# A bank of PSUM for every result from a list, and a new list of steps: attention and a feed-forward layer on one Trainium2 core

## The chip, the core and the metric

The kernel runs on one core of a Trainium2 chip. Its engines work side by side, each through its own list of instructions in order: TensorE (PE) multiplies matrices and writes only to PSUM, VectorE (DVE) and ScalarE (ACT) read PSUM and SBUF, GpSimd (POOL) works on SBUF, and SyncE (SP) issues nearly all DMAs. PSUM has 128 partitions and eight banks of 512 float32 values per partition; a result of a matmul here takes one bank or part of one. The metric is the device time of one execution in microseconds (us).

## The reference

`q`, `k` and `v` are (4, 8, 768, 64): four batches, eight heads, 768 positions. Attention sees a band of local positions and a few global ones, with a bias that grows with the distance; its output, 768 rows of 512 for each batch, goes through a layer norm and a feed-forward layer with a residual:

```python
scores = scale * np.matmul(q, k.transpose(0, 1, 3, 2))
keep = is_global | is_local                      # rel in [0, n_local) or key < n_global
scores = np.where(keep, scores + bias, -1e9)
a = softmax(scores)
x = (a @ v) as (B, S, H*D)                       # 4 x 768 x 512
xn = (x - mean) / sqrt(var + 1e-6) * g_ln
out = x + np.maximum(xn @ w_ch1, 0.0) @ w_ch2    # 512 -> 2048 -> 512
```

## The kernel before

The 24 tiles of 128 rows (four batches of six) are taken in an order of their own: the first tile of each batch comes first (tiles 0 to 3, float32 matmuls of 64 or 128 rows, function `first`), then the other 20 in pairs (`attention`, float16 parts, high and low). The feed-forward layer needs each weight as two float16 parts. `weight` loads 16 blocks of 1 MB, and each goes through two steps on ACT (L380, L388), two on DVE (L384, L392), a cast, and a subtraction (L403) that gives the low part. A product of high and low parts is three matmuls. Tiles 0 to 3 take their first layer alone in 16 results of 48 matmuls (`ffn1_alone`, L764 to L766); then come pairs with 256 columns (`ffn1`, L792 to L794), and from pair 4 on a scheme with seven products in place of eight (`seven`, L817 to L819, and `both_`, L954 and L973). `ffn2` (L1053) is the second layer of the early tiles.

Every piece of work is entered in a plan as a step on one engine with what it reads and writes. The order of the steps is a list of numbers, `STEPS`, and which engine takes a step that can go to several is a list, `HOMES`; both are written out in the file. The plan turns them into the instruction lists of the engines. Buffers (places in SBUF, banks in PSUM) are rings: the next user of a place waits until all users of the previous one are done.

PSUM's banks before are fixed by the kind of result, in turn: scores take banks 0 and 1 (`SS`), the outputs of attention banks 2 and 3, later 2 alone (`PVS`, `PVS2`), the first layer 4 and 5, later also 3 (`F1S`, `F1S2`), the second layer 6 and 7, and the transposes of the first tiles 6, 7 and 4 (`FLIPS`). The ring goes by the order in which the program enters the results.

At the start, while inputs and weights are on their way, PE gets fillers: matmuls of 252 columns on a constant tile, `still`, into the upper part of bank 3 (`hold`, L1174). Where the plan has PE free for a while and the planned time is under `HOLD`, it puts as many fillers there as fill 0.9 of the gap at 0.108 us each. They compute nothing that is used.

A flag that tells whether all ranges are in bounds is worked out near the end (`checks`, L1132 on PE, L1119 to L1122 on DVE); the steps after it stand in a block of their own, and a slower second kernel behind it (from L1427 on) runs only if the flag is set.

Of the kernel before, what the change touches and what calls it, by code (L numbers as in the profile page):

```python
# [18 lines left out]
ALU = mybir.AluOpType  # L19
# [4 lines left out]
B, H, S, D = 4, 8, 768, 64  # L24
DM, DF = 512, 2048
P = 128
NT = S // P
NK = DM // P
# [58 lines left out]
class Plan:  # L87
# [4 lines left out]
    def __init__(self):  # L92
        self.ops, self.wrote, self.read, self.rings, self.group = [], {}, {}, {}, None
# [55 lines left out]
    def order(self):  # L149
        for bufs, made in self.rings.values():  # L150
            for old, new in zip(made, made[bufs:]):
                for o in new.users:
                    if not any(p in new.users for p in o.before):
                        self.edges(old.users, o)
        assert sorted(STEPS) == list(range(len(self.ops)))
        self.planned = self.times([self.ops[n] for n in STEPS])
# [24 lines left out]
def banded(ctx, tc, q, k, v, n_global, n_local, g_ln, w1, w2, out, flag):  # L181
# [8 lines left out]
    plan = Plan()  # L190
# [56 lines left out]
    def psum(tag, of, shape):  # L247
        n_ = turn(tag, of)
        return plan.at([("ps", n_)], lambda: shaped(banks[n_], shape))
# [354 lines left out]
    def attention(t):  # L604
# [27 lines left out]
        for g_ in range(H // gh):  # L632
# [4 lines left out]
            def score(ps=ps, heads=heads):  # L637
                for u, h in enumerate(heads):
                    for n_ in range(nb):
                        for a in range(2):  # L640
                            pe.matmul(ps()[:, u, n_ * P:(n_ + 1) * P], lhsT=qT()[:, a * H + h, :], rhs=use[n_][0]()[:, h, :], start=(a == 0), stop=(a == 1))  # L641
# [112 lines left out]
    def ffn1_alone(t, j):  # L754
# [4 lines left out]
        def emit():  # L759
            for a in range(4):  # L760
                fs = slice((4 * j + a) % 8 * P, ((4 * j + a) % 8 + 1) * P)
                for kk in range(NK):
                    wh, wl = (block(j // 2, kk // 2)[:, part, kk % 2, fs] for part in range(2))
                    pe.matmul(ps()[:, a], lhsT=wh, rhs=xT()[:, 0, kk, :], start=(kk == 0), stop=False)  # L764
                    pe.matmul(ps()[:, a], lhsT=wh, rhs=xT()[:, 1, kk, :], start=False, stop=False)
                    pe.matmul(ps()[:, a], lhsT=wl, rhs=xT()[:, 0, kk, :], start=False, stop=(kk == NK - 1))  # L766
# [351 lines left out]
    def raised(pf):  # L1118
        vec.tensor_scalar(out=fine[:, 0:1], in0=pf()[:, 0:1], scalar1=float(P), scalar2=None, op0=ALU.is_ge)  # L1119
        vec.tensor_scalar(out=fine[:, 1:3], in0=pf()[:, 1:3], scalar1=1.0, scalar2=None, op0=ALU.is_ge)  # L1120
# [3 lines left out]
    def checks():  # L1124
# [6 lines left out]
        pf = plan.at([("ps", F1S2[0])], lambda: banks[F1S2[0]][0:1, 0:3])  # L1131
        op("PE", 0.1, lambda: pe.matmul(pf(), lhsT=ones, rhs=sums, start=True, stop=True), r=["ones", "sums"], w=[pf])  # L1132
# [83 lines left out]
IDLE, HOLD, FILL = 3, 130.0, 0.9  # L1216
# [15 lines left out]
HOMES = {32: 1, 50: 1, 53: 1, 68: 1, 115: 1, 147: 1, 153: 2, 154: 1, 167: 2, 175: 1, 182: 1, 188: 1, 189: 1, 196: 1, 203: 1, 210: 1, 230: 2, 231: 1,  # L1232
# [304 lines left out]
```

## Time and profile before

| | |
|---|---|
| time, median of 3 runs | 598.55 us (597.78 to 598.64) |
| the profiled execution: time, span | 598.57 us, 596.8 us (1.77 us lie around the span) |
| PE busy | 586.7 us, 98% of the span |
| DVE, ACT, POOL busy | 501.9 (84%), 334.1 (56%), 218.2 us (37%) |
| granted clock of PE, mean | 0.997 |
| fillers (L1174) | 151, the last at 52.9 us |
| all DMA queues | 91.74 MB, mean 154 GB/s |

A row of a matmul gives its start and a modelled end, and the next one starts long before that end: rows of 128 columns are 0.22 us long and start 0.055 us apart. So the busy share of PE hides gaps that are shorter than a row, and what PE really does is read from the starts.

### The profile page before, as it was taken

What the parts mean: (1) busy time and instruction counts of PE and PEld (TensorE: products, weight loads), DVE (VectorE), ACT (ScalarE), POOL (GpSimd) and SP (SyncE); (2) the same over time, 40 slices, a digit from 0 to 9 for tenths busy, and PEclk for the clock granted to TensorE, in tenths of its full rate; (3) what the DMA queues carried; (4) which work ended last, traced back from release to release, by engine and by line L of the source; (5) the groups of instructions that cost most, each with busy time, mean ns of one, the idle gap of its engine ahead of it and who ended that gap; (6) DMA issues with size and microseconds to landing.
All of it is one profiled execution on the core that took longest, in us unless ns stands there. A gap on an engine that the chain in (4) does not pass through costs nothing.

```text
span 596.8 us, 18645 instructions
## 1 busy us (share of the span) xinstructions
PE 586.7 (98%) x7657; PEld 513.6 (86%) x7657; DVE 501.9 (84%) x1147; ACT 334.1 (56%) x819; POOL 218.2 (37%) x228
## 2 busy tenths in 40 slices
PE   9899999999999999999999999999999999999995
PEld 7889988556877856899999999999999999999995
DVE  3999999989979988988987998888887997778661
ACT  4989788865644553753753762753664663551210
POOL 1315443245454253462332541341662441351200
PEclk9999999999999999999999999999999999999998
DMA  8896999996953878887989989978978796642201
GB/s 246 253 311 146 238 248 224 229 177 131 154 107 71 151 131 163 134 173 158 168 169 167 169 154 146 150 142 162 183 135 167 125 177 126 111 79 46 66 2 58
DMA packets 260269, 91.74 MB, mean 154 GB/s; under 512 B 250192, under 2 KB 250448, under 8 KB 260176
## 3 DMA queue, kind: packets, MB, share of 16 engines
q1 hardware_dynamic: 259888, 90.47, 77.0%
q8 instruction: 62, 1.02, 0.7%
q14 instruction: 31, 0.25, 0.2%
q10 hardware_dynamic: 288, 0.00, 0.0%
HBM read 38.01 MB, written 6.29 MB: 74 GB/s over the span
## 4 chain that ended last, share of the span: by engine, by line
PE 92%; DVE 4%; DMA 2%; ACT 1%; issue 0%; SPq 0%; DVEq 0%
PE bank L973 14%; PE bank L1053 14%; PE bank L954 12%; PE bank L817 8%; PE bank L819 8%; PE bank L818 8%; PE bank L641 6%; PE bank L794 2%; PE bank L792 2%; PE bank L793 2%; PE bank L1174 2%; PE bank L468 2%; PE bank L470 2%; PE bank L469 2%; PE bank L766 2%; PE bank L764 2%
## 5 line engine op out<-in xcount | busy, mean ns | idle before, releaser
L203 ACT ACTIVATE arena<-arena 128x512 f16<-128x512 f32 (+3 forms) x115 | 69.3, 619 | 54.3 <-DVE arena L716 13.8
L973 PE MATMUL bank<-w2h,arena 128*128 128x256 f16 x512 | 93.3, 273 | 0.0
L203 ACT ACTIVATE arena<-bank 128x512 f16<-128x512 f32 (+1 forms) x95 | 55.3, 591 | 67.1 <-PE bank L819 39.6
L819 PE MATMUL bank<-arena 128*128 128x128 f16 x512 | 87.9, 219 | 0.0
L818 PE MATMUL bank<-arena 128*128 128x128 f16 x512 | 87.9, 219 | 0.0
L817 PE MATMUL bank<-arena 128*128 128x128 f16 x512 | 87.9, 219 | 0.0
L505 ACT ACTIVATE arena<-arena,mn 128x256 f32<-128x256 f32 x160 | 80.0, 501 | 3.7
L1053 PE MATMUL bank<-w2h,arena 128*128 128x512 f16 x256 | 81.7, 379 | 0.0
L973 PEld LDWEIGHTS <-arena 128*128 128x128 f16 x768 | 73.0, 98 | 7.7
L973 PE MATMUL bank<-w2l,arena 128*128 128x256 f16 x256 | 69.8, 273 | 0.0
L954 PEld LDWEIGHTS <-arena 128*128 128x128 f16 x672 | 63.9, 98 | 6.8
L1053 PEld LDWEIGHTS <-arena 128*128 128x128 f16 x384 | 36.0, 98 | 37.4
L819 PE MATMUL bank<-arena,w 128*128 128x128 f16 x384 | 66.7, 219 | 0.0
L817 PE MATMUL bank<-arena,w 128*128 128x128 f16 x384 | 66.7, 219 | 0.0
L818 PE MATMUL bank<-arena,w 128*128 128x128 f16 x384 | 66.7, 219 | 0.0
L500 DVE CUSTOM_DVE_ANT_0 arena<-bank,mask 128x256 f32<-128x256 f32 x160 | 60.1, 417 | 7.4 <-PE bank L641 3.4
L647 POOL TENSOR_TENSOR arena<-arena 128x512 f16<-128x512 f32 x39 | 45.1, 1160 | 42.9 <-DVE r L476 10.6
L817 PEld LDWEIGHTS <-arena 128*128 128x128 f16 x512 | 50.1, 98 | 0.3
L818 PEld LDWEIGHTS <-arena 128*128 128x128 f16 x512 | 50.1, 98 | 0.3
L819 PEld LDWEIGHTS <-arena 128*128 128x128 f16 x512 | 50.1, 98 | 0.0
L1053 PE MATMUL bank<-w2l,arena 128*128 128x512 f16 x128 | 48.5, 379 | 0.0
L641 PE MATMUL bank<-kT,qT 128*128 128x128 f16 x640 | 47.2, 219 | 0.3 <-DMA qT<-qT 0.3
(215 smaller groups left out, 1773.1 us busy)
## 6 DMA issues: line engine op xcount, KB each, us to landing
arena<-in_moe_w_ch_dram SPq DMA_DIRECT2D x16, 1024.0 KB, 6.9
kf<-in_k_dram SPq DMA_DIRECT2D x28, 256.0 KB, 4.7
vf<-in_v_dram SPq DMA_DIRECT2D x28, 256.0 KB, 4.2
qf<-in_q_dram SPq DMA_DIRECT2D x24, 256.0 KB, 4.5
out_dram<-x SPq DMA_DIRECT2D x23, 256.0 KB, 2.5
qT<-qT SPq DMA_DIRECT2D x40, 128.0 KB, 3.5
pT<-arena SPq DMA_TRANSPOSE x80, 3.4
arena<-arena SPq DMA_TRANSPOSE x36, 3.2
```

Source lines behind the costliest of these rows:

```text
L203: act.activation(out=out(), in_=src(), func=AF.Relu if relu else AF.Copy, scale=by)
L468: pe.matmul(pv[:, h, :], lhsT=ph, rhs=vv[:, h, :D], start=(n_ == 0), stop=False)
L500: vec.tensor_tensor_reduce(out=T()[:, u, :], in0=ps()[:, u], in1=mask(h), scale=1.0 / Z, scalar=3e38, op0=ALU.add, op1=ALU.min, accum_out= ...
L505: act.activation(out=T()[:, u, :], in_=T()[:, u, :], func=AF.Exp, scale=-1.0, bias=mn()[:, h:h + 1], accum_out=sm()[:, h:h + 1])
L641: pe.matmul(ps()[:, u, n_ * P:(n_ + 1) * P], lhsT=qT()[:, a * H + h, :], rhs=use[n_][0]()[:, h, :], start=(a == 0), stop=(a == 1))
L647: pick(pair(lambda eng, pn=pn, T=T: eng.tensor_tensor(out=pn()[:, :, 1, :], in0=T(), in1=pn()[:, :, 0, :], op=ALU.subtract), 512, "PD"), r ...
L817: pe.matmul(ps()[:, i, :], lhsT=wh, rhs=xT()[:, hi + kk, :], start=(first_ and i == 0 and kk == 0), stop=False, skip_group_check=True)
L818: pe.matmul(ps()[:, i, :], lhsT=wh, rhs=xT()[:, lo + kk, :], start=False, stop=False, skip_group_check=True)
L819: pe.matmul(ps()[:, i, :], lhsT=wl, rhs=xT()[:, hi + kk, :], start=False, stop=(i == 3 and kk == 1), skip_group_check=True)
L954: pe.matmul(ps(), lhsT=hh()[:, part, f, :], rhs=rhs, start=first_ and f == 0 and k == 0, stop=(f == 3 and k == 2), skip_group_check=True)
L973: pe.matmul(ps(), lhsT=hh()[:, part, i, :], rhs=w[:, f + i, n * K2:(n + 1) * K2], start=False, stop=(i == 3 and k == 2), skip_group_check= ...
L1053: pe.matmul(ps[t](), lhsT=h[:, part, :], rhs=w[:, f + a, :], start=(f + a == 0 and n_ == 0), stop=(f + a == NF - 1 and n_ == 2))
```

## The change

Each result in PSUM, in the order in which the program enters it, gets its bank from a list `BANKS` of 257 numbers from 0 to 7. The ring of a bank is then ordered by the place of its results in `STEPS`, no longer by the order of entry. `STEPS` and `HOMES` are replaced as a whole. Since results that share a bank are now written from one `start` flag, scores and `ffn1_alone` set it on the first matmul of a bank only, and the check's small product takes the first row of a full buffer. `HOLD` goes from 130 to 75.

```diff
     def order(self):
-        for bufs, made in self.rings.values():
+        rank = {self.ops[n]: m for m, n in enumerate(STEPS)}
+        for key, (bufs, made) in self.rings.items():
+            if key[0] == "ps":
+                made = sorted((b for b in made if b.users), key=lambda b: min(rank[o] for o in b.users))
             for old, new in zip(made, made[bufs:]):
...
     def psum(tag, of, shape):
-        n_ = turn(tag, of)
-        return plan.at([("ps", n_)], lambda: shaped(banks[n_], shape))
+        n_ = BANKS[len(plan.banked)]
+        b = plan.at([("ps", n_)], lambda: shaped(banks[n_], shape))
+        plan.banked.append(b)
+        return b
...
-                            pe.matmul(ps()[:, u, n_ * P:(n_ + 1) * P], lhsT=qT()[:, a * H + h, :], rhs=use[n_][0]()[:, h, :], start=(a == 0), stop=(a == 1))
+                            pe.matmul(ps()[:, u, n_ * P:(n_ + 1) * P], lhsT=qT()[:, a * H + h, :], rhs=use[n_][0]()[:, h, :], start=(u == 0 and n_ == 0 and a == 0), stop=(u == gh - 1 and n_ == nb - 1 and a == 1), skip_group_check=True)
...
-        pf = plan.at([("ps", F1S2[0])], lambda: banks[F1S2[0]][0:1, 0:3])
+        pf = psum("pf", F1S2, [P, 3])
...
-IDLE, HOLD, FILL = 3, 130.0, 0.9
+IDLE, HOLD, FILL = 3, 75.0, 0.9
...
+BANKS = [
+    4, 1, 6, 2, 4, 7, 1, 0, 5, 3, 5, 3, 1, 7, 6, 4, 4, 7, 5, 2, 5, 7, 2, 1, 4, 6, 7, 5, 1, 7, 1, 3, 0, 3, 2, 5, 6, 2, 1, 5, 4, 5, 7, 0, 0, 6, 0, 2, 7, 1,
...
 STEPS = [
-    3, 2, 8, 5, 19, 23, 10, 6, 7, 9, 0, 1, 22, 21, 148, 141, 24, 25, 27, 155, 20, 80, 79, 17, 162, 84, 4, 12, 26, 13, 14, 28, 31, 33, 29, 15, 34, 32,
...
+    9, 7, 23, 81, 19, 5, 6, 8, 3, 2, 1, 0, 21, 22, 79, 80, 141, 27, 25, 4, 28, 12, 26, 29, 41, 13, 31, 33, 30, 14, 15, 16, 32, 42, 34, 87, 45, 89, 46,
```

The lists move instructions on every engine. Below stand three places, first as it was and then as it is. Names carry the bank (`bank6_78` is bank 6) and the tile; the new file's lines are 3 to 5 higher here (L197 is L200, L440 is L445).

PE, the third of the first loads (`q` and `k` of tile 2 are transposed, L440, the scores of tile 0 multiplied, L539, and its mask added, L543), before:

```order
L440 MATMUL bank6_78<-arena_71,qf2_0_128 128x128 x4
L539 MATMUL bank0_72<-k0_0_165,q0_0_187 128x128 x4
L440 MATMUL bank4_76<-arena_71,kf2_0_132 128x128 x4
L543 LDWEIGHTS arena_71
L543 MATMUL bank0_72<-arena_71 128x128
```

And changed:

```order
L445 MATMUL bank6_78<-arena_71,kf2_0_129 128x128 x4
L544 MATMUL bank1_73<-k0_0_189,q0_0_168 128x128 x4
L445 MATMUL bank2_74<-arena_71,qf2_0_133 128x128 x4
L544 MATMUL bank4_76<-k0_0_189,q0_0_168 128x128 x4
L548 LDWEIGHTS arena_71
L548 MATMUL bank1_73<-arena_71 128x128
```

Before, the second half of tile 0's scores (L539) comes after tile 1's and uses bank 0 again; now it follows at once in bank 4. Along the whole list of PE, the fillers fall from 151 to 72; up to the first matmul of `ffn1_alone` there are 148 before and 70 now, and all other matmuls of the main program are the same in number and shape.

DVE, the first reductions of the scores (L549) and what stands between them, before:

```order
L199 TENSOR_SCALAR q0_1_228<-bank6_78 128x512
L549 TENSOR_REDUCE nm0_236<-bank0_72 128x4
L549 TENSOR_REDUCE nm1_262<-bank1_73 128x4
L549 TENSOR_REDUCE nm0_236<-bank0_72 128x4
L197 COPY pT0_0_285<-bank7_79 128x512
L384 TENSOR_SCALAR arena_71<-arena_71 128x1024
```

And changed:

```order
L202 TENSOR_SCALAR q0_1_244<-bank2_74 128x512
L554 TENSOR_REDUCE nm0_260<-bank1_73 128x4
L554 TENSOR_REDUCE nm0_260<-bank4_76 128x4
L554 TENSOR_REDUCE nm1_288<-bank0_72 128x4
L200 COPY k0_2_292<-bank5_77 128x512
L554 TENSOR_REDUCE nm1_288<-bank7_79 128x4
L200 COPY pT0_1_312<-bank1_73 128x512
L389 TENSOR_SCALAR arena_71<-arena_71 128x1024
```

Before, three reductions come out of two banks; now four come out of four. The first step on a weight (L384, now L389) moves from fifth to seventh behind the copy of `q`.

SP, the loads after the first two, before:

```order
L269 DMA qf2_0_128<-in_q_dram 128x8x64
L269 DMA kf2_0_132<-in_k_dram 128x8x64
L372 DMA arena_71<-in_moe_w_ch1_dram 128x2x512 x2
L520 DMA vf1_124<-in_v_dram 128x8x64
L372 DMA arena_71<-in_moe_w_ch1_dram 128x2x512
L520 DMA vf0_122<-in_v_dram 128x8x64
L269 DMA qf1_0_185<-in_q_dram 128x8x64
L269 DMA kf1_0_193<-in_k_dram 128x8x64
```

And changed:

```order
L274 DMA kf2_0_129<-in_k_dram 128x8x64
L274 DMA qf2_0_133<-in_q_dram 128x8x64
L274 DMA kf1_0_135<-in_k_dram 128x8x64
L274 DMA qf1_0_137<-in_q_dram 128x8x64
L377 DMA arena_71<-in_moe_w_ch1_dram 128x2x512 x2
L525 DMA vf0_121<-in_v_dram 128x8x64
L377 DMA arena_71<-in_moe_w_ch1_dram 128x2x512
L525 DMA vf1_116<-in_v_dram 128x8x64
```

`q` and `k` of the third tile (0.25 MB each) move ahead of the first two weights (1 MB each). At the other end of SP's list the last DMA of the main program was half a row block of tile 23 (L991, 128 KB) and is a whole one of tile 22 (L998, 256 KB); PE's last products were tile 23's and are tile 22's.

## Rows read from the trace of the kernel before

**Rows 1.** The page: busy time, share of the span and instructions of each engine.

```profile
PE 586.7 (98%) x7657; PEld 513.6 (86%) x7657; DVE 501.9 (84%) x1147; ACT 334.1 (56%) x819; POOL 218.2 (37%) x228
```

**Rows 2.** Windows, PE alone: stretch, PE busy, granted clock, DMA share, GB/s.

```profile
0.00:25.00 25.00, 22.49 (x173) 1.00 0.89 253
25.00:50.00 25.00, 24.44 (x266) 1.00 0.87 246
50.00:75.00 25.00, 24.29 (x381) 1.00 0.93 219
75.00:150.00 75.00, 75.00 (x840) 1.00 1.00 200
450.00:575.00 125.00, 125.00 (x1850) 1.00 0.55 103
```

**Rows 3.** Waits of PE: line, waited for, us in total, times, longest.

```profile
PE bank L1174 <- DVE x L579: 1.5, 2, 1.0
PE bank L766 <- POOL w L403: 0.4, 1, 0.4
PE bank L641 <- DMA qT<-qT: 0.3, 1, 0.3
```

**Rows 4.** Timeline of PE: start, us, line, count; start, middle and end of the span.

```profile
0.98 3.75 PE L1174 MATMUL bank<-still 128*128 128x252 bf16 x17 [0.98 <-DVE still L1205]
4.68 1.09 PE L440 MATMUL bank<-arena,kf 128*128 128x128 f32 x4
5.56 1.59 PE L1174 MATMUL bank<-still 128*128 128x252 bf16 x9
6.99 0.60 PE L440 MATMUL bank<-arena,qf 128*128 128x128 f32 x4
7.43 1.15 PE L1174 MATMUL bank<-still 128*128 128x252 bf16 x9
...
29.98 2.02 PE L1174 MATMUL bank<-still 128*128 128x252 bf16 x17
31.84 0.63 PE L440 MATMUL bank<-arena,kf 128*128 128x128 f32 x4
...
44.64 0.22 PE L764 MATMUL bank<-arena,w 128*128 128x128 f16 x1
44.69 0.22 PE L765 MATMUL bank<-arena,w 128*128 128x128 f16 x1
44.75 0.22 PE L766 MATMUL bank<-arena,w 128*128 128x128 f16 x1
...
77.06 0.38 PE L1053 MATMUL bank<-w2l,arena 128*128 128x512 f16 x1
77.28 0.59 PE L1053 MATMUL bank<-w2h,arena 128*128 128x512 f16 x2
...
590.24 0.27 PE L973 MATMUL bank<-w2h,arena 128*128 128x256 f16 x1
```

**Rows 5.** The chain that ended last, two of its links: start, us, engine, line, count.

```profile
551.96 2.62 PE bank L954 x24
586.58 3.94 PE bank L973 x36
```

**Rows 6.** Timeline of DVE: waits for PE at the start, six rows in sequence, the last weight.

```profile
10.94 0.69 DVE L549 TENSOR_REDUCE nm<-bank 128x4 f32<-128x512 f32 x1 [0.67 <-PE bank L543]
13.12 0.69 DVE L549 TENSOR_REDUCE nm<-bank 128x4 f32<-128x512 f32 x1 [1.48 <-PE bank L543]
14.75 0.69 DVE L549 TENSOR_REDUCE nm<-bank 128x4 f32<-128x512 f32 x1 [0.94 <-PE bank L543]
...
43.49 1.26 DVE L403 TENSOR_TENSOR w<-arena,w 128x1024 f16<-128x1024 f32 x1
44.66 1.33 DVE L384 TENSOR_SCALAR arena<-arena 128x1024 uint16<-128x1024 uint16 x1
45.78 0.66 DVE L549 TENSOR_REDUCE nm<-bank 128x4 f32<-128x512 f32 x1
46.36 0.67 DVE L197 COPY pT<-bank 128x512 f32<-128x512 f32 x1
...
120.13 1.23 DVE L403 TENSOR_TENSOR w2l<-arena,w2h 128x1024 f16<-128x1024 f32 x1
```

**Rows 7.** The page, DMA issues of the output: count, KB each, median us to landing.

```profile
out_dram<-x SPq DMA_DIRECT2D x23, 256.0 KB, 2.5
out_dram<-x SPq DMA_DIRECT2D x2, 128.0 KB, 1.7
```

More of the change, by code (lines that the diff above doesn't have):

```diff
@@ L92, in __init__ @@
     def __init__(self):
-        self.ops, self.wrote, self.read, self.rings, self.group = [], {}, {}, {}, None
+        self.ops, self.wrote, self.read, self.rings, self.group, self.banked = [], {}, {}, {}, None, []
     def ring(self, name, bufs, make):
@@ L763, in emit @@
                     wh, wl = (block(j // 2, kk // 2)[:, part, kk % 2, fs] for part in range(2))
-                    pe.matmul(ps()[:, a], lhsT=wh, rhs=xT()[:, 0, kk, :], start=(kk == 0), stop=False)
-                    pe.matmul(ps()[:, a], lhsT=wh, rhs=xT()[:, 1, kk, :], start=False, stop=False)
-                    pe.matmul(ps()[:, a], lhsT=wl, rhs=xT()[:, 0, kk, :], start=False, stop=(kk == NK - 1))
+                    pe.matmul(ps()[:, a], lhsT=wh, rhs=xT()[:, 0, kk, :], start=(a == 0 and kk == 0), stop=False, skip_group_check=True)
+                    pe.matmul(ps()[:, a], lhsT=wh, rhs=xT()[:, 1, kk, :], start=False, stop=False, skip_group_check=True)
+                    pe.matmul(ps()[:, a], lhsT=wl, rhs=xT()[:, 0, kk, :], start=False, stop=(a == 3 and kk == NK - 1), skip_group_check=True)
         names = [f"1_{j}_{c_}{e}" for c_ in range(2) for e in "hl"]
@@ L1118, in raised @@
     def raised(pf):
-        vec.tensor_scalar(out=fine[:, 0:1], in0=pf()[:, 0:1], scalar1=float(P), scalar2=None, op0=ALU.is_ge)
-        vec.tensor_scalar(out=fine[:, 1:3], in0=pf()[:, 1:3], scalar1=1.0, scalar2=None, op0=ALU.is_ge)
+        vec.tensor_scalar(out=fine[:, 0:1], in0=pf()[0:1, 0:1], scalar1=float(P), scalar2=None, op0=ALU.is_ge)
+        vec.tensor_scalar(out=fine[:, 1:3], in0=pf()[0:1, 1:3], scalar1=1.0, scalar2=None, op0=ALU.is_ge)
         vec.tensor_reduce(out=every, in_=fine, axis=AX.X, op=ALU.min)
@@ L1130, in checks @@
         op("DVE", 0.5, verdict, r=[("mv", t) for t in range(B * NT)], w=["ok", "sums"])
-        pf = plan.at([("ps", F1S2[0])], lambda: banks[F1S2[0]][0:1, 0:3])
-        op("PE", 0.1, lambda: pe.matmul(pf(), lhsT=ones, rhs=sums, start=True, stop=True), r=["ones", "sums"], w=[pf])
+        pf = psum("pf", F1S2, [P, 3])
+        op("PE", 0.1, lambda: pe.matmul(pf()[0:1, 0:3], lhsT=ones, rhs=sums, start=True, stop=True), r=["ones", "sums"], w=[pf])
         op("DVE", 0.6, lambda: raised(pf), r=[pf], w=["flag"])
@@ L1231 @@
 SUMS = (*G, list(range(20, 24)))
-HOMES = {32: 1, 50: 1, 53: 1, 68: 1, 115: 1, 147: 1, 153: 2, 154: 1, 167: 2, 175: 1, 182: 1, 188: 1, 189: 1, 196: 1, 203: 1, 210: 1, 230: 2, 231: 1,
[19 rows of a table removed]
+HOMES = {26: 1, 28: 1, 32: 1, 56: 1, 75: 1, 88: 1, 147: 1, 153: 2, 154: 1, 160: 2, 161: 1, 175: 1, 189: 1, 203: 1, 217: 1, 231: 1, 263: 1, 272: 1,
[19 rows of a table added]
+BANKS = [
[5 rows of a table added]
+]
 TMPS = [28, 27]
```

218 rows, old and new, of tables (BANKS, HOMES, STEPS) are left out of this document.

## The prediction

> **What bounds the kernel now.** I read the busy times first: PE is busy for 98% of the span, DVE for 84% [rows 1]. [...] Third, the waits of PE: three rows of DVE, POOL and DMA that together are 2.2 us [rows 3], in a span of 597. Fourth, the starts of single matmuls, since the modelled ends cover gaps. A matmul of 128 columns follows the one before by 0.055 to 0.06 us, one of 512 by 0.22 [rows 4], and 24 of 256 take 2.62, or 0.109 each [rows 5]. In the chain the last 36 stand end to end (3.94 us) [rows 5].
>
> With these I add up what PE has to do, the fillers left out: 4096 matmuls of 128 columns by 0.0556, 228 us; 1824 of 256 by 0.109, 199; 384 of 512 by 0.216, 83; 960 of 64 by 0.029, 28; and 27 us for the float32 transposes and products of the first four tiles and their masks. That is 564 us, and the change leaves all of it. PE's last matmul starts at 590.24 [rows 4] and so ends its issue at 590.35. PE therefore lost 26 us: 16.2 to 151 fillers (31.84 less 29.98 for 17 of them is 0.109 with rounding [rows 4]; 0.107 over all), and 10 to standing still. Since the windows have no gap after 75 us, nearly all of the 26 lie before that. This is the whole prize; what happens to banks at 300 us can only cost.
>
> **What lost the 26 us.** At the start there is no work: PE starts at 0.98, waits for the first load until 4.68 with 17 fillers between (1.9 us still), and stands 0.44 and 0.45 us around the next nine fillers [rows 4], in all 3.7 us. Afterwards it waits on results in few banks: scores of four half tiles go through banks 0 and 1, and a filler that writes bank 3 waits for DVE to read an attention result out of the same bank, 1.5 us in two waits [rows 3]. DVE waits for PE in turn, 0.67, 1.48 and 0.94 us in three rows [rows 6].
>
> **The change, part by part.**
>
> Fillers: 151 become 72, that is 79 by 0.107, 8.5 us off PE's list. They are free only if work takes their place or the wait behind them goes; that is the rest of the sum. The lowered `HOLD` takes none away by itself: the last stands far below 75 us in both lists.
>
> Start: the three first blocks of fillers (17, 9 and 9) and the three first loads are as they were in number and size, so the 3.7 us and 3.8 us of fillers stay. Then the changed list puts 24.0 us of real work ahead of the first matmul of `ffn1_alone`, with 70 fillers (7.5 us); before it is 21.2 us of work and 148 fillers (15.9), and the matmul starts at 44.64 [rows 4]. The work moved up is the transposes and scores of tile 2, whose loads go ahead of the weights. SP's list is moved by 0.5 MB, at the 253 GB/s of the first window [rows 2] 2 us for the first two weights. I cost this at nothing, since DVE reaches the first step of the first weight 1.2 us later in its new list anyway (two rows of 0.6); if the cover is gone, it is the 2 us.
>
> The pace of the weights: this is the term I can bound from both sides. DVE has to work through its list in order until the low part of the last of 16 weights is there. I add the list up to that row with the distances of starts: 1.15 for a subtraction or shift of 1024, 1.11 for the first step, 0.6 for an eviction, a reduction or a copy of 512 [rows 6], and so on. Before it comes to 104.6 us, changed to 105.2. Before, the row ends at 121.3 [rows 6], so DVE had not worked for 16.7 us, 5.5 of them before its inputs came. PE first reads this weight after 97.6 us of real work before, 123.6 with the 26 lost: it was ready 2.3 us earlier. In the changed list 105.4 us of real work stand ahead of it. If DVE idles for D, the weight is ready at 105.2 + D, and PE must have lost at least D - 0.2 by then. D as before gives 16.5 us lost. The lower end does not come from DVE: the 7.7 us of the 72 fillers and the 3.7 of the start are 11.4. I take 14, the middle, because the three waits of DVE for PE [rows 6], 3.1 us, are just those that more banks dissolve (16.7 less 3.1 is 13.6), while ACT's part of each weight stays what it was.
>
> The later stretch: PE had no gap there [rows 2], so no bank can give anything; I cost it at nothing. Whether it takes something I counted from the lists: places after the first 100 us where PE writes a bank again with under 1.5 us of its own work since the matmuls that the reader of the bank waited for. There are 52 before and 35 now. Two readers of 512 columns are 0.67 us each [rows 6], so these are the places that could stall; before they did not. If the cover is gone, one costs about 0.5 us. The moves of casts between ACT, DVE and POOL change DVE's total by some rows in 1147; DVE has 16% of the span free [rows 1].
>
> The end: from PE's last matmul to the end of the span are 6.45 us. The last DMA now has 256 KB in place of 128, which land after 2.5 in place of 1.7 us [rows 7]: plus 0.8, bounded by 0 and 0.9.
>
> The sum against the profiled execution (596.8 us of span, 598.57 in all, 0.02 above the median): 564 of work, 14 lost, 6.45 of end, 0.8 more, and 1.77 around the span: **587.0 us**, 11.6 less.
>
> On the clock the rows show 1.00 in the first window too, where PE was busy for 22.49 of 25 us with its fillers [rows 2]. [...]
>
> **The rivals.**
>
> (A) DVE sets the pace as before: the weights are no earlier than their sum allows with the same 16.7 us of idling. For it speaks that DVE's sum is the same to 0.6 us and that it was at work for 90% of that stretch; against it, that part of its idling was for PE. PE loses 16.5: 589.5 us. A variant is that PE stands still for 10 us as before beside the fewer fillers: 17.7 lost, 590.7.
>
> (B) All of the fillers turn into waits, since what they covered is the arrival of loads: the bytes are the same and DMA runs at 89% in the first window [rows 2]. PE loses 26 again and the end is longer: 599.4 us, no change by the bound. Against it: more real work stands ahead of the same loads.
>
> [...]
>
> (D) Slower: short turnarounds stall at last. 35 places by 0.5 us are 17.5 us, 604.5; it decides above 0.33 us per place. Against it are the 52 places of before without a gap.
>
> (E) The lists don't do what they say because a wait is hidden in a ring: the banks' rings now go by the place in `STEPS`, so no result can wait for a later one. I give it no chance of its own.
>
> **How the numbers follow.** Forecast 0.57 (583 to 589.2), A 0.26, B 0.07, C 0.05, D 0.05. The low end is the floor of 11.4 us lost without the longer DMA: 583.6, rounded down by 0.6 for what the sum of 564 may be off. The high end takes in A and its variant and 2 us for the first weights, up to 593.5. Less than 0.2% (1.2 us) can't be told from no change. Faster by more than that are the forecast and A, and a part of B, C and D where the fall is small: 0.86; same: most of B, 0.05; slower: C and D and the rest of B, 0.09.
>
> **What the profile would show.** If right: the first matmul of `ffn1_alone` starts at 35 to 38 us instead of 44.64; the row of the last weight's low part ends at 117 to 120; PE's windows are full from about 75 us; PE's last matmul is at 576 to 580, with a granted clock of 1.00 in the first window. A is right if that DVE row ends at 121 to 122 and PE waits for it. B would show the first `ffn1_alone` at 44 again with waits on DMA or DVE where the fillers were. [...] The forecast is wrong if PE has a gap after 150 us, or if the last matmul comes later than 583.

## The result, and the profile after

The changed kernel takes 589.28 us (median of four: 590.48, 589.69, 588.87, 588.65) against 598.31 beside it, a ratio of 0.9852 with an interval of 0.9833 to 0.9871. Timed again later it took 590.00 (ratio 0.9870, 0.9845 to 0.9895). The forecast was 587.0 with a range of 583.0 to 593.5: direction and range hold, and the median is 2.3 to 3 us later.

The page and PE's windows of the changed kernel, which answer to [rows 1, 2]. The profiled execution is the slowest of the four: 590.48 us, 588.7 of them span.

```profile
PE 578.9 (98%) x7578; PEld 507.2 (86%) x7578; DVE 498.5 (85%) x1149; ACT 333.6 (57%) x818; POOL 222.5 (38%) x227
```

```profile
0.00:25.00 25.00, 23.91 (x189) 1.00 0.92 243
25.00:50.00 25.00, 23.23 (x266) 0.93 0.87 274
50.00:75.00 25.00, 25.00 (x446) 1.00 0.75 202
75.00:150.00 75.00, 75.00 (x762) 1.00 0.98 201
150.00:300.00 150.00, 149.50 (x1816) 1.00 0.85 150
300.00:450.00 150.00, 150.00 (x2237) 1.00 0.91 159
```

PE is full from 50 us on but for half a microsecond near 293, where before it was not until 75. One stretch is new: from 25 to 50 us it is busy for 23.23 us only, and the granted clock is 0.93, where before it was 1.00. PE's own rows show where (columns as in [rows 4]; lines after the new code are 3 to 12 higher than before, so L764 is L769 here):

```profile
36.25 0.22 PE L769 MATMUL bank<-arena,w 128*128 128x128 f16 x1
...
38.93 1.95 PE L572 MATMUL bank<-vf,pT 128*128 128x65 f32 x16
42.33 0.66 PE L445 MATMUL bank<-arena 128*128 128x128 f32 x4 [1.45 <-ACT arena L206]
...
42.99 0.31 PE L771 MATMUL bank<-arena,w 128*128 128x128 f16 x1
43.10 0.31 PE L769 MATMUL bank<-arena,w 128*128 128x128 f16 x1
43.21 0.31 PE L770 MATMUL bank<-arena,w 128*128 128x128 f16 x1
...
581.95 0.27 PE L978 MATMUL bank<-w2h,arena 128*128 128x256 f16 x1
```

The first matmul of `ffn1_alone` comes at 36.25 instead of 44.64. Those 8.4 us are the gain: PE's last matmul is 8.3 us earlier. But some four microseconds after 36.25 PE stands still for 1.45 us for tile 2's normed row, whose transposes are L445, and then its matmuls follow each other by 0.107 us instead of 0.055, while the granted clock is 0.50. The windows bound that stretch:

```profile
40.00:42.00 2.00, 0.88 (x8) 1.00 0.97 358
42.00:44.00 2.00, 1.67 (x16) 0.71 1.04 397
44.00:46.00 2.00, 2.00 (x22) 0.50 0.83 242
46.00:48.00 2.00, 2.00 (x36) 0.93 0.12 32
```

The wait near 293 us is one for a bank that DVE has to read first:

```profile
293.08 0.27 PE L959 MATMUL bank<-w2h,arena 128*128 128x256 f16 x1 [0.50 <-DVE x L485]
```

PE's last matmul starts at 581.95 (590.24 before) and the span ends 6.64 us after its issue. With 564 us of work, PE lost 18.1 us, where it lost 26 before and 14 were forecast.

What PE waits for stands on three engines, in the order of time: DVE's row that takes off the mean and multiplies by the gain (L595), POOL's power (`rs`, 128 elements of one column), ACT's scaling with it. DVE in its turn then waits for ACT's step on the next weight.

```profile
38.15 0.97 DVE L595 SCALAR_TENSOR_TENSOR arena<-x,mv,gb 128x512 f32<-128x512 f32 x1
39.04 2.45 DVE L389 TENSOR_SCALAR arena<-arena 128x1024 uint16<-128x1024 uint16 x2
...
43.43 1.23 DVE L397 SCALAR_TENSOR_TENSOR arena<-arena 128x1024 int32<-128x1024 int32 x1 [1.95 <-ACT arena L393]
```

```profile
34.30 4.27 POOL L408 TENSOR_TENSOR w<-arena,w 128x1024 f16<-128x1024 f32 x2
38.52 3.00 POOL L497 TENSOR_TENSOR rs<-rs,half 128x1 f32<-128x1 f32 x1
```

```profile
41.56 0.72 ACT L206 ACTIVATE arena<-arena,rs 128x512 f32<-128x512 f32 x1 [1.92 <-POOL rs L497]
```

The power takes 3.00 us; the other 23 rows of the same line take 0.55 to 1.10. It ends at 41.52, just after DVE's two 16-bit steps L389 (41.49).

Earlier, DVE still waits for PE to finish scores, three times as before [rows 6]:

```profile
14.43 0.69 DVE L554 TENSOR_REDUCE nm<-bank 128x4 f32<-128x512 f32 x1 [1.27 <-PE bank L548]
...
16.32 0.69 DVE L554 TENSOR_REDUCE nm<-bank 128x4 f32<-128x512 f32 x1 [0.61 <-PE bank L548]
...
19.85 0.69 DVE L554 TENSOR_REDUCE nm<-bank 128x4 f32<-128x512 f32 x1 [0.51 <-PE bank L548]
```

### The profile page after: what moved, and what is told of

The parts are those of the page before. It is cut to its first block, busy times and chain, and to the rows that moved or that the text cites. A ratio compares the mean times of both kernels' runs of the same rounds, so it can differ in the third digit from the quotient of the medians.

```text
span 588.7 us, 18462 instructions
## 1 busy us (share of the span) xinstructions
PE 578.9 (98%) x7578; PEld 507.2 (86%) x7578; DVE 498.5 (85%) x1149; ACT 333.6 (57%) x818; POOL 222.5 (38%) x227
## 4 chain that ended last, share of the span: by engine, by line
PE 90%; DVE 2%; issue 0%; ACT 0%; DVEq 0%
PE bank L1058 14%; PE bank L978 14%; PE bank L959 12%; PE bank L822 8%; PE bank L824 8%; PE bank L823 8%; PE bank L646 6%; PE bank L770 2%; PE bank L798 2%; PE bank L799 2%; PE bank L797 2%; PE bank L771 2%; PE bank L769 2%; PE bank L473 2%; PE bank L475 2%; PE bank L474 1%
## 5 line engine op out<-in xcount | busy, mean ns | idle before, releaser
L206 ACT ACTIVATE arena<-arena 128x512 f16<-128x512 f32 (+3 forms) x120 | 73.4, 624 | 71.6 <-DVE arena L838 16.6
L978 PE MATMUL bank<-w2h,arena 128*128 128x256 f16 x512 | 92.7, 273 | 0.0
L206 ACT ACTIVATE arena<-bank 128x512 f16<-128x512 f32 (+1 forms) x85 | 49.5, 593 | 48.3 <-PE bank L824 26.1
L652 POOL TENSOR_TENSOR arena<-arena 128x512 f16<-128x512 f32 x42 | 48.5, 1159 | 53.7 <-ACT arena L206 15.2
L959 PE MATMUL bank<-w2h,arena 128*128 128x256 f16 x256 | 47.1, 273 | 0.5 <-DVE x L485 0.5
```

Source lines behind the costliest of these rows:

```text
L206: act.activation(out=out(), in_=src(), func=AF.Relu if relu else AF.Copy, scale=by)
L652: pick(pair(lambda eng, pn=pn, T=T: eng.tensor_tensor(out=pn()[:, :, 1, :], in0=T(), in1=pn()[:, :, 0, :], op=ALU.subtract), 512, "PD"), r ...
L959: pe.matmul(ps(), lhsT=hh()[:, part, f, :], rhs=rhs, start=first_ and f == 0 and k == 0, stop=(f == 3 and k == 2), skip_group_check=True)
L978: pe.matmul(ps(), lhsT=hh()[:, part, i, :], rhs=w[:, f + i, n * K2:(n + 1) * K2], start=False, stop=(i == 3 and k == 2), skip_group_check= ...
```

## The experiments

Theory at the start: the gain is the start-up (real work in place of fillers and waits), and the 2 to 3 us over the forecast are this wait and the half clock behind it. Rival: DVE's pace of the weights sets the end (A of the prediction). Medians of the kernel before lie at 598.18 to 598.21 in all of them.

**The power ahead of POOL's subtraction.** `STEPS.remove(161); STEPS.insert(STEPS.index(128) + 1, 161)`, and `HOLD` 40 for 75, which takes away the last two fillers.

> Only one step moves: on POOL the power of tile 2's moments goes ahead of the second of the two 2.1 us subtractions that stood before it (the low part of block w1_1_0), and the two fillers planned at 47 us are gone (70 left). Theory (the lost time is the wait at 40.7 us and the lower clock after it): the power starts when DVE has the moments, at about 37.5, and takes 0.6 to 1.3 us as in its other rows; the transposes of xT2 follow the products of tile 1 or 2 without the 1.6 us of standing still; the granted clock stays at 1.00 from 42 to 47 us (it was 0.50); PE's lost sum falls from 18.1 to about 14.5, the last matmul comes at 578.5, the time is 585.8 +- 0.8. Rival A (DVE's pace of weights sets the end): the gain is no more than the last weight's low part comes earlier (DVE itself waited 1.95 us for ACT at 43.4), so at most 2 us, 587.4 to 589.3, and PE stands still for that weight near 118 to 121 us. A third reading, that the power is slow wherever it stands beside any DVE work: it still takes about 3 us and nothing changes (589.3).

589.71 us, ratio 0.9854 (0.9840 to 0.9867): no gain. The power is short now, but DVE's next row is not (DVE, then POOL):

```profile
38.30 2.70 DVE L595 SCALAR_TENSOR_TENSOR arena<-x,mv,gb 128x512 f32<-128x512 f32 x1
```

```profile
37.78 0.55 POOL L497 TENSOR_TENSOR rs<-rs,half 128x1 f32<-128x1 f32 x1 [1.15 <-ACT arena L206]
38.30 2.15 POOL L408 TENSOR_TENSOR w<-arena,w 128x1024 f16<-128x1024 f32 x1
```

L595 takes 2.70 us instead of 0.97: it starts with the subtraction and ends 0.55 us after it. The wait has changed hands, and PE still stands 0.82 us at the same place. It also met waits for DVE at 45.5 and 48.9 us (0.19 and 0.20 us) that were not there before: it was ahead of two low parts that DVE makes, tile 2's and that of weight w1_1_1.

**DVE's two 16-bit steps later.** Steps 164, 171, 165, 172 and 166 go behind 133 (xT2's low part, that of tile 2's transposed row); `HOLD` 40.

> POOL's list stays; DVE's two first steps (16-bit, 1.2 us each) of weights w1_1_1 and w1_2_0 go behind the low part of xT2 (with them ACT's and DVE's next steps of these two weights), and the two fillers planned at 47 us are gone. Nothing of DVE then stands beside POOL's power at 38.5. If DVE's 16-bit rows are what stretched the power from 0.6 to 3.0 us: it takes 0.6 to 1.0, xT2's transposes start at about 40.4 and PE does not stand still, clock 1.00. If the power is slow for another reason (it follows a 2.1 us subtraction on POOL, or the row is rough): it still takes about 3 us and the wait stays. On the time: the two weights come some 1.5 to 2.5 us later and with them all of DVE's list to the last weight (row ends at 121 to 122 instead of 120.1). Theory (PE's lost work sets the time, the weights have about 3 us of slack): 586 to 588. Rival A (the pace of weights sets it): 590.5 to 592.

591.50 us, 0.9887 (0.9872 to 0.9903). The power now takes 1.00 us and the transposes start at 40.77 without a wait (POOL, then PE):

```profile
38.58 1.00 POOL L497 TENSOR_TENSOR rs<-rs,half 128x1 f32<-128x1 f32 x1
```

```profile
40.77 0.60 PE L445 MATMUL bank<-arena 128*128 128x128 f32 x4
```

Without L389 beside it the power is short, so L389 is what stretched it. But PE then waits 1.6 and 1.1 us for the two weights:

```profile
PE bank L769 <- ACT w L206: 1.6, 1, 1.6
PE bank L771 <- DVE w L408: 1.1, 1, 1.1
```

So the weights did not have the 3 us of slack here that the theory gave them, and the time is in the rival's range. Part of the median may be the clock's: the profiled execution (590.09) has a mean clock of 0.997, the other three (591.40 to 591.78) 0.994 or 0.995.

**More DVE work ahead of the last weights.** In the first step of a weight: `for _ in range(2 if n in (12, 13) else 1):` around the 16-bit operation; `HOLD` 40.

> DVE's first step of two weights of w2 (numbers 12 and 13 of 16) is done twice, the same result over again: 2 x 1.15 us more in DVE's list ahead of the last weight's low part, nothing else changed but the two fillers at 47 us, which are gone. Theory: the last weight was ready at 120.1 and PE first read it about 2 to 3 us later, so the time stays at 589.3 +- 0.7 and PE has no wait there. Rival A (pace of weights sets the end): 2.3 us more, 591.6, with a wait of PE for DVE's L408 near 121 us.

592.14 us, 0.9904 (0.9886 to 0.9922), 2.1 to 2.9 us more than the changed kernel: the theory's "no change" is wrong and the rival's number right. The wait is not for the last weight but for the two ahead of it (PE in the kernel with more DVE work):

```profile
116.19 0.38 PE L1059 MATMUL bank<-w2l,arena 128*128 128x512 f16 x1 [1.72 <-DVE w2l L409]
...
120.89 0.38 PE L1059 MATMUL bank<-w2l,arena 128*128 128x512 f16 x1 [0.22 <-DVE w2l L409]
```

The same two matmuls in the changed kernel, and the rows of DVE that they need:

```profile
114.16 0.38 PE L1058 MATMUL bank<-w2l,arena 128*128 128x512 f16 x1
...
118.49 0.38 PE L1058 MATMUL bank<-w2l,arena 128*128 128x512 f16 x1
```

```profile
112.43 1.24 DVE L408 TENSOR_TENSOR w2l<-arena,w2h 128x1024 f16<-128x1024 f32 x1
...
117.18 1.21 DVE L408 TENSOR_TENSOR w2l<-arena,w2h 128x1024 f16<-128x1024 f32 x1
118.92 1.21 DVE L408 TENSOR_TENSOR w2l<-arena,w2h 128x1024 f16<-128x1024 f32 x1
```

Weight 13 is there at 113.67 and read at 114.16, weight 14 at 118.39 and read at 118.49. A wait view that names no DVE hides a slack of 0.5 and 0.1 us.

**No fillers after the first three blocks.** `HOLD` 9.

> The changed kernel with no fillers after the first three blocks: 37 fewer (2, 7, 16, 7 and 3 at 19 to 30 us, 2 at 47 us), 35 left. If the fillers only stand where PE would stand still, its real work starts at the same times: the first matmul of ffn1_alone at 36.2 as now, and the time stays at 589.3 +- 0.7 as long as the clock does. The theory says that PE's gap of 1.9 us at 23.7 (18 fillers now) has the same effect as the gap of 1.6 us at 40.7: the granted clock falls to 0.50 for about 3.5 us after it, and matmuls there run at half pace; some 1.5 us more, 590 to 592. [...] If fillers stand in the way of real work: 1 to 3 us less, 586.5 to 588.5.

591.78 us, 0.9875 (0.9852 to 0.9899). The clock falls and stays low:

```profile
16.00:24.00 8.00, 7.23 (x65) 1.00 1.01 265
24.00:32.00 8.00, 6.93 (x37) 0.59 0.97 320
32.00:40.00 8.00, 8.00 (x45) 0.50 1.05 282
40.00:48.00 8.00, 8.00 (x99) 0.84 0.79 279
```

`ffn1_alone` starts at 40.95, 4.7 us later, and 2.5 us of that are left in the median. The time is in the range of the theory, though the clock is low for far longer than its 3.5 us. Matmul by matmul, this kernel is 5.5 us behind the changed one at 40 us and 2.0 behind at 50: the wait of 1.45 us for tile 2 and the half clock after it, which the profile of the changed kernel has in between, are not in this one. The one execution with a mean clock of 0.993 took 589.02 us, the three with 0.983 to 0.986 took 591.68 to 592.89, so the fillers here seem to be worth what they do to the clock.

**Less DVE work, alone and with the power first.** `few = 16 if n in (12, 13) else 1024`, and `[:, :few, 1]` in the same operation; the second kernel has the first experiment's move too.

> Leaves out part of the computation: DVE's first step of two weights of w2 (numbers 12 and 13 of 16), which sets the sign of the low words, is done on 16 of 1024 elements (the mirror of the run that did it twice). DVE has 2 x 1.1 us less ahead of the low parts of weights 13 to 15. After the first four runs the theory reads: two limits end nearly together, PE's lost time in the start and DVE's pace of the weights; in the changed kernel the low parts of weights 13 and 14 were ready 0.5 and 0.1 us before PE read them (rows ending 113.67 and 118.39). By it the less work of DVE alone gives nothing, since PE is not there earlier: 588.5 to 589.5, the rows of the last low parts 2 us earlier, no wait of PE for them. If DVE's pace alone sets the end: 587.0 +- 0.5.

589.02 us, 0.9853 (0.9833 to 0.9873): as the two limits had it. Low parts 13 to 15 end 1.6 to 1.9 us earlier, and nothing that can be told from the changed kernel (589.28, later 590.00) comes of it.

> Leaves out the same part, and has POOL's power of tile 2 ahead of the subtraction, as in the run with the power first. By two limits that end together, only the two together help: PE gains the 1.6 us that the power gave up to 63 us and does not give them back to waits for the weights: 586.5 to 587.8, the last matmul at about 580. If DVE's pace alone sets the end: 587.0, the same as with less DVE work alone. If PE's start alone sets it: the same as with the power first alone, 589.3 +- 0.6.

588.85 us, 0.9846 (0.9833 to 0.9860). Not the 586.5 to 587.8 that two limits should give, nor any difference that can be told from less DVE work alone. Weights 13 to 15 are not all that PE meets on the dot. In its trace, long before them, PE waits 0.17, 0.21 and 0.19 us for DVE at 45.3, 48.7 and 66.1 us (tile 2's low part, the low part of w1_1_1, and a low part ahead of a later tile's scores, L647). Compared with the changed kernel's profile matmul by matmul, it is 1.7 us ahead at 65 us and 1.3 at 90; with less DVE work alone 1.7 and 0.7, with the power first alone 1.6 and 0.5. So part of what the start gives is lost again well ahead of weight 13; the waits that show there are those of the scores (L646, L647 here): 0.25 and 0.23 us with the power first, 0.30 with less DVE work.

**The banks alone.** The list, engines and `HOLD` of before, and in `BANKS` for each result the bank that has been free longest. Fillers write into bank 3 while results of more than 260 columns lie there, which changes part of those; no instruction is left out.

> The kernel before with its own list of steps, its own engines for the copies and its own 152 fillers; only the banks change: each result takes the bank of the eight that has been free longest by the place of its steps in that list. No engine's order moves. Theory (banks give nothing as long as the order of the steps stays, they only make room for another order): the waits of fillers and scores for a bank, some 1.5 us, go, and come back as the next wait; 596.5 to 599 against 598.2. Rival (the banks themselves are the gain): 589 to 592, with the waits of DVE for PE near 29, 42 and 57 us gone.

598.49 us, 1.0002 (0.9993 to 1.0011): nothing. `ffn1_alone` starts at 44.48, as it did [rows 4]; PE's waits for DVE's attention result [rows 3] are gone, and others of 1.1 and 0.8 us stand at the fillers (the row of 1.0 is the start, as before):

```profile
PE bank L1179 <- ACT pT L206: 1.1, 1, 1.1
PE bank L1179 <- DVE still L1210: 1.0, 1, 1.0
PE bank L1179 <- DVE nm L554: 0.8, 1, 0.8
```

**The new list with the old banks in the start.** `n_ = BANKS[len(plan.banked)] if len(plan.banked) >= 36 else turn(tag, of)`, and a loop in `order` that moves a step behind what it needs.

> The changed kernel, but the first 36 results, all of the four start tiles, are in the fixed banks for each kind as before (scores 0 and 1, attention results 2 and 3, transposes 6, 7 and 4); the other 207 keep their own. A step that would come ahead of the last user of its bank is moved behind it (201 places of 2319 differ, all in the first 295). The program plans 244 fillers instead of 72, since PE has to wait for banks. Theory (the gain of the change is made by the banks of the first 40 us): the first matmul of ffn1_alone comes 10 to 14 us later than 36.25, and the end with it, less what slack the weights have: 598 to 603. Rival (the gain comes from the later stretch or from the list without the banks): 589 to 593.

626.30 us, 1.0466 (1.0447 to 1.0486). `ffn1_alone` starts at 58.23, 22 us later than in the changed kernel, and at 101.9 us PE waits 4.4 us for a bank that DVE has to empty. The direction is as expected, both sizes are far larger. Of the 37 us above the changed kernel, 18.4 are 172 more fillers by 0.107. A searched list was not made for these banks, so the 37 us are not the worth of the banks. What the pair of runs shows is that neither part, put into a kernel without the other, gives the gain; what the best list for the old banks would take is open, and so is what the new engines (`HOMES`) and the earlier loads are worth by themselves.

**DVE waits for the power.** In `tied`: the 16-bit step of w1_1_1 depends on the power of tile 2; `HOLD` 40. No order moves.

```diff
+        if n == 128:
+            power[:] = [new[-1].name]
+            return
+        if n == 164:
+            tc.add_manual_dep(new[0], power.pop(), SYNC, reason="port")
```

> The changed kernel with one dependence more: DVE's first step of w1_1_1 (16 bits, the first of the two that stand beside POOL's power of tile 2) waits for that power. No engine's order moves; the two fillers at 47 us are gone (70 left). From the earlier runs: the power took 3.0 us beside the two steps and 1.0 without them, and when the power went ahead of POOL's subtraction, that subtraction held up DVE's L595 instead (2.70 us for 0.97). [...] Rival (the weights behind it are the limit whatever happens at 40 us, as in the run with the power first): 588.8 to 589.7.

588.53 us (588.03 to 590.28), 0.9842 (0.9819 to 0.9865), 1.5 us below the changed kernel beside it (590.00), 0.75 below its first median (589.28), and 0.27 below the rival's range. The intervals overlap, so a gain in time is likely and not shown. Its rows (DVE, POOL, PE):

```profile
38.20 0.98 DVE L595 SCALAR_TENSOR_TENSOR arena<-x,mv,gb 128x512 f32<-128x512 f32 x1
39.62 2.51 DVE L389 TENSOR_SCALAR arena<-arena 128x1024 uint16<-128x1024 uint16 x2 [0.44 <-POOL rs L497]
```

```profile
38.57 1.02 POOL L497 TENSOR_TENSOR rs<-rs,half 128x1 f32<-128x1 f32 x1
```

```profile
39.00 1.95 PE L572 MATMUL bank<-vf,pT 128*128 128x65 f32 x16
40.79 0.61 PE L445 MATMUL bank<-arena 128*128 128x128 f32 x4
...
579.58 0.27 PE L978 MATMUL bank<-w2h,arena 128*128 128x256 f16 x1
```

A wait of 0.44 us added to DVE takes away the one of 1.45 on PE and all but 0.17 of the 1.95 on DVE itself, and the last matmul comes at 579.58, within the 576 to 580 of the forecast. The low part of w1_1_1 ends at 47.57 instead of 48.69; DVE's row here, then in the changed kernel:

```profile
46.30 1.27 DVE L408 TENSOR_TENSOR w<-arena,w 128x1024 f16<-128x1024 f32 x1
```

```profile
47.42 1.27 DVE L408 TENSOR_TENSOR w<-arena,w 128x1024 f16<-128x1024 f32 x1
```

By its median this is the fastest kernel of the study. The kernel's own plan already keeps such rows apart: steps marked `port` never overlap in it, and a marked step of POOL is made to wait for the marked step of DVE ahead of it. The power is not marked, and no step of DVE is made to wait for POOL in this way; the dependence above adds that in one place.

**The changed kernel again, and with its gap filled.** The second has 15 more fillers ahead of tile 2's transposes (`n += 15 * (o is plan.ops[131])`, `HOLD` 40).

> The changed kernel itself, unchanged, beside the other two. 588.6 to 590.5 as before; if the clock's fall after the gap at 40.7 us comes in some executions and not in others, as the profiles say (it fell to 0.50 in the changed kernel and in the run with more DVE work, and not in the one with less, all with the same wait of 1.45 us), the times fall in two groups about 1.5 us apart, with a mean clock of 0.994 in the slower.

590.00 us. In its profile PE stands 1.49 us at the same place, and the clock stays at 1.00 behind it. Of four profiles with that wait (the changed kernel's two, more and less DVE work; 1.45 to 1.49 us) it fell in two. The two executions with a mean clock of 0.994 took 590.06 and 590.62, three with 0.996 or 0.997 took 589.42, 589.50 and 589.94: some 0.7 us apart, not 1.5. (The sixth, 593.33 at 0.996, fits neither.) Among the first four, the one at 0.994 (590.48) is 1.4 us above the mean of the other three.

> The changed kernel with 15 fillers (1.6 us) in PE's gap at 40.7 us, ahead of xT2's transposes, and without the two at 47 us: 85 in all. The wait itself stays. If the gap is what lets the clock fall: it stays at 1.00 from 42 to 47 us in every execution, no time is above 589.3, and the median is 588.8 +- 0.3. If the clock's fall has another cause: the same two groups as in the kernel without them, median 589.3. If the low part of w1_1_1 (48.7 us) is what binds next, the gain over an execution with the fall is less than the 1.7 us that the half clock takes.

590.16 us, 0.9868 (0.9848 to 0.9888). The clock is 1.00 from 38 to 50 us, 0.998 in the mean of the profiled execution, and the time no better. Against the profile with the half clock, PE is 1.6 us ahead at 62 us and 0.5 at 68; in between it waits 0.87 us for a transposed query:

```profile
66.05 1.12 PE L646 MATMUL bank<-kT,qT 128*128 128x128 f16 x17 [0.87 <-DMA qT<-qT]
```

So the half clock does not explain the median.

## Why the prediction was right, and where it was off

*Where the time comes from: right.* The 26 us that PE lost were the prize, nearly all of it before 75 us, and 8 to 9 of them are back. `ffn1_alone` starts at 36.25 (35 to 38 forecast), the fillers are 72, PE has no gap from 50 us but one of half a microsecond near 293. No bank pays at 300 us, and rival D's stalls are this one place, not 35. By the letter of the prediction such a gap after 150 us proves it wrong; it is worth 0.5 us and is not in the second profile. That neither half of the change, put into a kernel without the other, gives the gain (1.0002, 1.0466) was not forecast; it fits a start that is a chain through all engines. The first steps on the first weight (ACT's L385 at 16.24 us, DVE's L389 at 17.57) wait for no load, so costing the moved loads at nothing was right.

*The term that was off: "I take 14" lost.* PE lost 18.1 us in the profiled execution and 17.0 in the second profile (its last matmul starts at 580.88), so its last matmul is not at the 576 to 580 forecast. By the prediction's own prices (24.0 us of work ahead of `ffn1_alone`, 105.4 ahead of the last weight), 12.25 us were lost when `ffn1_alone` began at 36.25, and 16.1 when PE first read the last weight at 121.53; 2.0 more went after that. An estimate from the distances of starts puts 3.5 of the 3.9 in the middle before 50 us: the wait of 1.45, the half clock, two fillers. Of the 2.0 at the end, the gap near 293 is 0.7; the rest is a pace slightly slower than the prices. The kernel before has that too: it read the last weight at 122.72, not at 123.6, so the weight was ready 1.4 us earlier and not 2.3. The prediction took a loss up to the last weight for the whole loss. Besides, two steps of the working failed.

First, the bound was made with the last weight alone. DVE's row of it ends at 120.13 (121.36 before [rows 6]; 117 to 120 forecast), so DVE idled 14.9 us (the prediction's D) on a list of 105.2, close to the 13.6 to 14 taken; PE did not wait for it. The reason given for the 14 mostly failed: DVE's three waits for PE, said to dissolve, are 2.4 us where they were 3.1. But weights 13 and 14 were there only 0.5 and 0.1 us before they were read, and 2.3 us more of DVE work ahead of them cost 2.1 to 2.9. "PE must have lost at least D - 0.2" was treated as the price, though it is only one of sixteen lower bounds. The last weight is there 1.4 us before it is read and weight 14 only 0.1, so a bound from weight 14 at the same D would have been 1.3 us higher. Yet in the changed kernel PE waits for no weight after 50 us, and less DVE work (589.02) gave nothing that can be told. So rival A, DVE's pace, is not what set the time; it is the next limit, 0.1 us away, at other weights than the one it named. Its 589.5 came nearer than 587.0 without its signs (that row at 121 to 122, PE waiting for it), which is partly luck.

Second, the chain of tile 2 was costed at nothing. The power that stands beside DVE's two steps took 3.00 us instead of 1.0, PE stood for it, ACT's and DVE's part of the next weight waited with it (1.92 and 1.95 us), and one dependence that keeps them apart takes the wait away. By the medians it brings 0.75 to 1.5 us, a third to a half or a little more of what the forecast missed, and that is not clear of the noise.

*The end: too dear.* 6.64 us instead of 7.25; the end is 0.2 us longer than before, not 0.8.

*Small slips that changed nothing.* The view of PE's waits before has five rows with 3.7 us in all, not three with 2.2. The upper bound of 593.5 is 0.8 above what it is said to be made of (590.7 and 2).

*Rivals.* B did not come: 72 fillers, and no waits on loads in place of the others. The 0.05 of C stood for a lower clock ahead of `ffn1_alone`; that was the author's estimate, and no row of before shows such a clock. In the changed kernel the windows have 1.00 up to 42 us, and 0.50 came behind the wait of 1.45 us, in some executions. Those took 0.7 and 1.4 us longer in the two sets of runs, but the kernel with the gap filled, whose profile has 1.00 there, was no faster (590.16). The kernel without the later fillers had a low clock ahead of `ffn1_alone`, 0.59 from 24 to 32 us and 0.50 from 32 to 40, and took 591.78.

## What to carry to other kernels

Where one engine makes what another reads in a row of pieces, bound the reader by every piece, not by the last: slack of 0.1 us shows in no view of waits until something moves. Freeing the banks paid here only with the order that it permits (0.9852, the banks alone 1.0002), so search both together. And a small operation on the critical chain wants a place where the other engine is not in the way: here, moving it or the long one only changed who waited, and a dependence that held the other engine back for 0.44 us cost least (588.53, against 589.71 and 591.50).

## What the runs showed of the hardware

POOL and DVE held each other up, in both directions: POOL's power of 128 elements took 3.00 and 3.02 us beside DVE's two 16-bit steps (the changed kernel, and with its gap filled) and 1.00 and 1.02 without them (0.55 at its shortest), and DVE's L595 took 2.70 us beside POOL's subtraction, against 0.97. The long row ended 0.03 us (the power, in the changed kernel) and 0.55 us (L595) after the other engine's. Why they hold each other up, no run shows.

The clock fell to 0.50 after a wait of 1.45 us of PE in two of four profiles, and not in the two others with the same wait (1.45 and 1.49 us). While it was 0.50, matmuls of 128 columns started 0.107 us apart instead of 0.055.
